# Scaled float16 halves for the second expert's input layer, with its x tiles loaded and scaled in groups of four

## The chip, the cores and the metric

The kernel runs on one core of one Trainium2 chip. The metric is the device time of one execution in microseconds (us). The engines are PE (TensorE: matmuls, with its weight loads shown apart as PEld), DVE (VectorE), ACT (ScalarE), POOL (GpSimd) and SP (SyncE, which issues the DMAs here).

## The reference

Three layers follow each other: block-causal attention (8 batches, 8 heads, 576 positions, head size 64), an expert with an ELU, and a second expert with a softmax-weighted unit and a layer norm. The diff touches the first product of the last one.

```python
x = attn_out.transpose(0, 2, 1, 3).reshape(4608, 512)
x = elu(x @ w_in) @ w_out                     # first expert, d_ff 2048
h = x @ w_in2                                 # second expert, d_ff 1024
e = exp(h - max(h)); sm = e / (sum(e) + 1e-9)
solu = h * sm
ln = (solu - mean(solu)) / sqrt(var(solu) + 1e-6) * g_ln
out = ln @ w_out2                             # [4608, 512], float32
```

The weights come in as 64-bit floats and are decoded to float32 on the chip.

## The kernel before

**Products in halves.** A float32 operand is split into a high and a low half, and a product of two operands is three matmuls: high by high, high by low and low by high. In attention, in the first expert and in the last product (`g4`, L1579) the halves are float16, scaled by a power of two or a bound on the values beforehand; in the second expert's input layer (`g3`, L1516) they are float32r, without a scale.

**The second expert.** It works on 36 tiles of 128 tokens. For a tile, SP loads x from the DRAM buffer `x2d` (`x_load`, L1499), ACT and DVE split it (`x_hi` L1504, `x_lo` L1508), and PE runs `g3`: 24 matmuls of 128x512. Then come `s_max` (L1523, DVE), `s_exp` (L1529, ACT), `s_solu` (L1534 to L1538, DVE), `s_var` (L1544, ACT), `s_rstd` (L1552, POOL), `s_ln` (L1556, DVE), `s_hi` and `s_lo` (L1561 on POOL, L1565 on DVE), and a transposing DMA (`s_tr`, L1571). Three tiles later `g4` (24 float16 matmuls of 128x512) multiplies the transposed halves with `w_out2`; ACT evicts (`o_ev`, L1587) and SP stores.

**Weights of the second expert.** While PE works on the last batches of the first expert, eight blocks are decoded: four of `w_in2` (`w3_*`) and four of `w_out2` (`w4_*`). A block is loaded into one of two buffers `r`, and goes through `dec_abs` (L773, ACT), `dec_sign` (L777, POOL), `dec_clamp` (L780, DVE) and `dec_bits` (L784 and L785, DVE) into a float32 block in one of two buffers `t3`. Of `w_in2`, each block is then split at once (`w3_hi` L1446 on ACT, `w3_lo` L1449 on DVE). Of `w_out2`, each block is multiplied by `g_ln` (L1468), reduced (`w4_amax`, L1472), the reductions are summed over the partitions by a small float32 matmul with ones (`over_partitions`, L285, a pair of PE instructions), DVE makes the scale (`w4_scale`), and the block is split (L1486, L1490).

**First expert.** `g1` (L683) makes eight pieces of a half batch, 24 matmuls each; ACT, DVE and POOL turn a piece into the float16 halves of G (L693, L695, L738, L742, L747), and `g2` (L757) needs pieces 0 to 3 for its first and 4 to 7 for its second half of the contraction.

**Order.** All instructions are issued in an order that a planner in the kernel works out when the kernel is built. Each operation has a cost, a due time (`nom`) and what it depends on; the planner keeps a clock for each engine and gives an engine that comes free, of the operations that could start first, the one with the lowest due time. Buffers and PSUM slots are rings (`Ring`); `rM` holds the four PSUM slots that all matmul groups share. The order is fixed: on the chip an engine waits where its next operation is not ready. The operations of the second expert have later due times than all of the first one's.

```python
rX, rXH, rXL, rE2, rSQ, rHL, rLT, rOS = Ring(2), Ring(2), Ring(2), Ring(3), Ring(2), Ring(2), Ring(LAG + 1), Ring(3)
```

Of the kernel before, what the change touches and what calls it, by code (L numbers as in the profile page):

```python
# [8 lines left out]
F32 = mybir.dt.float32  # L9
F32R = mybir.dt.float32r  # L10
# [22 lines left out]
LAG = 3  # L33
# [70 lines left out]
class Plan:  # L104
# [5 lines left out]
    def op(self, eng, cost, fn, nom, *deps, lat=0.12, dma=0.0):  # L110
        o = Op(eng, cost, fn, nom, deps, lat, dma, len(self.ops))
        self.ops.append(o)
        return o
# [87 lines left out]
def kernel(  # L201
# [732 lines left out]
    def cA(n, ap=1, acc=0, psum=False):  # L934
        return (0.834 * n + (52 if psum else 93) + 93 * ap + 93 * acc) / 1e3
# [475 lines left out]
    def open_p2():  # L1411
        es_att.close()
        w = ctx.enter_context(tc.tile_pool(name="p2w", bufs=1))
        p2["w3h"] = w.tile([128, 4, 1024], F32R, name="w3h")
        p2["w3l"] = w.tile([128, 4, 1024], F32R, name="w3l")
        p2["w4"] = w.tile([128, 8, 2, 512], F16, name="w4")
        p2["gl"] = w.tile([128, 8], F32, name="gl")
        p2["c4"] = w.tile([128, 3, 4], F32, name="c4")
        p2["mh"] = w.tile([128, 1], F32, name="mh")
        p2["px"] = w  # L1420
        p2["es_st"] = ExitStack()
        p2["st"] = p2["es_st"].enter_context(tc.tile_pool(name="p2st", bufs=1))
        SP.dma_start(out=p2["gl"], in_=g_ln.rearrange("(k p) -> p k", p=128))
# [9 lines left out]
        SP.dma_start(out=r, in_=w_in2.bitcast(I32)[128 * i:128 * i + 128].rearrange("p (f w) -> p f w", w=2))  # L1433

    def w3_abs(i):
        p2["t3", i] = p2["st"].tile([128, 1024], F32, name="t3", tag="t3", bufs=2)
        dec_abs(p2["t3", i], p2["r3", i])

    def w3_clamp(i):
# [2 lines left out]
    def w3_dec(i):  # L1442
        dec_bits(p2["t3", i], p2["r3", i])

    def w3_hi(i):
        A.activation(out=p2["w3h"][:, i], in_=p2["t3", i], func=AF.Copy, scale=1.0)  # L1446

    def w3_lo(i):
        V.tensor_tensor(out=p2["w3l"][:, i], in0=p2["t3", i], in1=p2["w3h"][:, i].bitcast(F32), op=ALU.subtract)  # L1449

    def w4_load(i):
        r = p2["st"].tile([128, 8, 128, 2], I32, name="r", tag="r", bufs=2)
# [1 line left out]
        SP.dma_start(out=r, in_=w_out2.bitcast(I32)[:, 256 * i:256 * i + 256].rearrange("(k p) (f w) -> p k f w", p=128, w=2))  # L1454

    def w4_abs(i):
        p2["t4", i] = p2["st"].tile([128, 8, 128], F32, name="t3", tag="t3", bufs=2)
        dec_abs(p2["t4", i], p2["r4", i])

    def w4_clamp(i):  # L1460
# [29 lines left out]
        V.scalar_tensor_tensor(out=p2["w4"][:, :, 1, 128 * i:128 * i + 128], in0=p2["t4", i], scalar=p2["c4"][:, 1, i:i + 1],  # L1490
                               in1=p2["w4"][:, :, 0, 128 * i:128 * i + 128], op0=ALU.mult, op1=ALU.subtract)

    x_t, h_t = {}, {}
    XB = 128

    def x_load(j):
        px = p2["px"]
        x = px.tile([128, 4, XB], F32, name="x", tag="x", bufs=2)
        SP.dma_start(out=x, in_=x2d[:, XB * j:XB * j + XB].rearrange("(k p) n -> p k n", p=128))  # L1499
        x_t[j] = [x, None, None]  # L1500

    def x_hi(j):
        x_t[j][1] = p2["px"].tile([128, 4, XB], F32R, name="xh", tag="xh", bufs=2)
        A.activation(out=x_t[j][1], in_=x_t[j][0], func=AF.Copy, scale=1.0)  # L1504

    def x_lo(j):
        x_t[j][2] = p2["px"].tile([128, 4, XB], F32R, name="xl", tag="xl", bufs=2)
        V.tensor_tensor(out=x_t[j][2], in0=x_t[j][0], in1=x_t[j][1].bitcast(F32), op=ALU.subtract)  # L1508

    def g3(i, slot):  # L1510
        _, xh, xl = x_t[i]
# [8 lines left out]
    def s_max(i):  # L1520
        d = h_t[i]
        d["mx"] = sm(1, "mx2")
        V.tensor_reduce(out=d["mx"], in_=d["h"], axis=AX.X, op=ALU.max, negate=True)  # L1523

    def s_exp(i):
        d = h_t[i]
        d["e"] = p2["wk"].tile([128, 1024], F32, name="e2", tag="e2", bufs=3)
        d["su"] = sm(1, "su2")
        A.activation(out=d["e"], in_=d["h"], func=AF.Exp, bias=d["mx"], scale=1.0, accum_out=d["su"])  # L1529

    def s_solu(i):
        d = h_t[i]
        r = sm(1, "r2")
        V.tensor_scalar(out=r, in0=d["su"], scalar1=1e-9, scalar2=None, op0=ALU.add)  # L1534
        V.reciprocal(out=r, in_=r)
        d["mu"] = sm(1, "mu")
        V.scalar_tensor_tensor(out=d["e"], in0=d["e"], scalar=r, in1=d["h"], op0=ALU.mult, op1=ALU.mult, accum_out=d["mu"])
        V.tensor_scalar(out=d["mu"], in0=d["mu"], scalar1=-1.0 / 1024.0, scalar2=None, op0=ALU.mult)  # L1538
# [60 lines left out]
        o = op("SP", DMA_IN, lambda: fn(i), nom, o_open, d, dma=dL(1048576))  # L1599
        return o, rR.users[-1]  # L1600

    w3_end, w4_end, prev = [], [], {}
    for i in range(8):
        z = i % 4
        t_ = t + 6 * i
        l, users = plan_load(w3_load if i < 4 else w4_load, z, t_ - 7)
        fa, fc, fd = (w3_abs, w3_clamp, w3_dec) if i < 4 else (w4_abs, w4_clamp, w4_dec)
        a_ = op("ACT", cA(1024, 0), lambda z=z, fa=fa: fa(z), t_, l, prev.get(i - 2))
        sg = op("Pool", 1.55, lambda z=z, i=i: dec_sign(p2["r3" if i < 4 else "r4", z]), t_ + 0.4, a_)
        x = op("DVE", 0.7, lambda z=z, fc=fc: fc(z), t_ + 0.5, a_)  # L1610
        x = op("DVE", 3.0, lambda z=z, fd=fd: fd(z), t_ + 1, x, sg)
        users += [a_, x]
        if i < 4:
            h = op("ACT", cA(1024, 0), lambda z=z: w3_hi(z), t_ + 4, x)
            lo = op("DVE", cV(1024, 0), lambda z=z: w3_lo(z), t_ + 5, h)
            w3_end += [h, lo]
        else:
            x = op("DVE", cV(1024, 0), lambda z=z: w4_g(z), t_ + 3, x, o_open)
            x = op("DVE", cV(1024, 0), lambda z=z: w4_amax(z), t_ + 4, x)
            x, users2 = plan_all(lambda y, z=z: w4_all(z, y), t_ + 5, x)  # L1620
            x = op("DVE", 0.7, lambda z=z: w4_scale(z), t_ + 5.5, x)
            users2.append(x)
            h = op("ACT", cA(1024, 1), lambda z=z: w4_hi(z), t_ + 6, x)
            lo = op("DVE", cV(1024, 1), lambda z=z: w4_lo(z), t_ + 7, h)
            w4_end += [h, lo]
        prev[i] = [h, lo]
    all_g2 = [x2_ops[b] for b in range(B)]
    t = tick(28 + 16 * 7) + 16 * TICK1
    o_openw = op("Pool", 0.01, open_wk, t, all_g2)
    rX, rXH, rXL, rE2, rSQ, rHL, rLT, rOS = Ring(2), Ring(2), Ring(2), Ring(3), Ring(2), Ring(2), Ring(LAG + 1), Ring(3)  # L1630
    xs_op = {}

    def plan_x(j, nom):
        lo_b, hi_b = (XB * j) // S, (XB * j + XB - 1) // S
        d = rX.take()
        l = op("SP", DMA_IN, lambda: x_load(j), nom - 10, o_open, d, [x2_ops[b] for b in range(lo_b, hi_b + 1)], dma=dL(512 * XB))
        d = rXH.take()
        h = op("ACT", cA(4 * XB, 0), lambda: x_hi(j), nom - 5, l, d)
        d = rXL.take()
        lo = op("DVE", cV(4 * XB, 0), lambda: x_lo(j), nom - 4, h, d)  # L1640
        rX.use(h, lo)
        xs_op[j] = lo

    T2 = 10.8
    g4s = []

    def plan_g4(i, nom):
# [6 lines left out]
        dz.users.append(ev)  # L1654
        rOS.use(op("SP", DMA_IN, lambda: o_st(i), nom + 6, ev, dma=dL(262144)))

    plan_x(0, t)
    for i in range(NTILE):
        nom = t + T2 * i
        if i + 1 < NTILE:  # L1660
            plan_x(i + 1, nom + T2)
        d = rM.take()
        mm = op("PE", 5.57, lambda i=i, d=d: g3(i, d), nom, xs_op[i], w3_end, d, chain[-1:])
        rXH.users[i].append(mm)
        rXL.users[i].append(mm)
        hu = d.users
# [62 lines left out]
```

## Time and profile before

| what | value |
|---|---|
| median of 3 runs | 1514.84 us (1513.22 to 1521.68) |
| profiled execution | 1522.49 us, of which the span from first to last instruction is 1520.7 us |
| mean granted clock of TensorE | 0.972 of full speed |
| busy: PE, DVE, ACT, POOL | 1444.7, 1052.5, 812.6, 536.3 us |
| busy of PE's weight loads (PEld) | 1022.1 us |

The busy share is a mean over stages with different limits. Matmuls are pipelined: one that is shown as busy for 379 ns can start its successor long before it ends, so a step is read from start to start or from the chain that ended last. Idle time counts only on the engine that sets the end.

### The profile page before, as it was taken

What the parts mean: (1) busy time and instruction counts of PE and PEld (TensorE: products, weight loads), DVE (VectorE), ACT (ScalarE), POOL (GpSimd) and SP (SyncE); (2) the same over time, 40 slices, a digit from 0 to 9 for tenths busy, and PEclk for the clock granted to TensorE, in tenths of its full rate; (3) what the DMA queues carried; (4) which work ended last, traced back from release to release, by engine and by line L of the source; (5) the groups of instructions that cost most, each with busy time, mean ns of one, the idle gap of its engine ahead of it and who ended that gap; (6) DMA issues with size and microseconds to landing.
All of it is one profiled execution on the core that took longest, in us unless ns stands there. A gap on an engine that the chain in (4) does not pass through costs nothing. (4 is left out here: it accounts for less than half of the span.)

```text
span 1520.7 us, 31276 instructions
## 1 busy us (share of the span) xinstructions
PE 1444.7 (95%) x12266; PEld 1022.1 (67%) x12268; DVE 1052.5 (69%) x1946; ACT 812.6 (53%) x1712; POOL 536.3 (35%) x631
## 2 busy tenths in 40 slices
PE   6888898999999999999999999989999999999998
PEld 3455565686777677678668667858776666666664
DVE  5879899878697787868868677597217555555552
ACT  4678666657475575565746656444414343333332
POOL 5677567444243343434424334242102111111110
PEclk9888799999999999999999999989999999999999
DMA  9235566856656576577565645530005444444433
GB/s 273 55 98 124 124 133 125 156 110 130 131 104 118 110 128 129 96 138 142 95 140 92 116 87 90 169 126 10 15 25 118 96 98 100 95 102 98 99 83 76
DMA packets 500130, 165.62 MB, mean 109 GB/s; under 512 B 445712, under 2 KB 492816, under 8 KB 499472
## 3 DMA queue, kind: packets, MB, share of 16 engines
q1 hardware_dynamic: 499984, 163.64, 50.7%
q8 instruction: 96, 1.57, 0.4%
q14 instruction: 50, 0.41, 0.1%
HBM read 63.44 MB, written 18.87 MB: 54 GB/s over the span
## 5 line engine op out<-in xcount | busy, mean ns | idle before, releaser
L683 PE MATMUL m<-XT,WIN 128*128 128x320 f16 (+1 forms) x3072 | 402.0, 289 | 10.5 <-DVE pwi L848 5.4
L757 PE MATMUL m<-G,WOUT 128*128 128x320 f16 (+1 forms) x3072 | 404.9, 291 | 5.2 <-POOL G L742 2.2
L683 PEld LDWEIGHTS <-WIN 128*128 128x128 f16 x3072 | 298.1, 99 | 96.1 <-issue 16.7
L757 PEld LDWEIGHTS <-WOUT 128*128 128x128 f16 x3072 | 298.8, 100 | 92.8 <-issue 8.7
L521 POOL TENSOR_SCALAR PN<-e,r 128x384 f16<-128x384 f32 (+2 forms) x280 | 184.7, 673 | 263.0 <-DVE r L503 120.3
L497 ACT ACTIVATE e<-m,nb,cqk 128x256 f32<-128x256 f32 (+4 forms) x252 | 159.7, 640 | 134.4 <-DVE nb L480 116.2
L742 POOL TENSOR_SCALAR G<-rp,sg 128x640 f16<-128x640 f32 (+1 forms) x128 | 126.6, 990 | 248.4 <-DVE rp L738 135.5
L693 ACT ACTIVATE rp<-m,ch 128x512 f32<-128x512 f32 (+1 forms) x256 | 176.4, 738 | 67.1 <-PE m L683 52.3
L1579 PE MATMUL m<-w,lt 128*128 128x512 f16 x864 | 192.2, 379 | 0.0
L526 DVE SCALAR_TENSOR_TENSOR PN<-e,r,PN 128x384 f16<-128x384 f32 (+2 forms) x280 | 172.3, 653 | 17.7 <-POOL PN L521 17.6
L1579 PEld LDWEIGHTS <-lt 128*128 128x128 f16 x864 | 81.9, 98 | 103.3 <-issue 8.9
L747 DVE SCALAR_TENSOR_TENSOR G<-rp,sg,G 128x640 f16<-128x640 f32 (+1 forms) x128 | 119.7, 938 | 26.2 <-POOL G L742 25.9
L476 DVE TENSOR_REDUCE mx<-m 128x2 f32<-128x768 f32 (+3 forms) x128 | 101.6, 814 | 44.5 <-PE m L452 37.8
L1552 POOL TENSOR_TENSOR rs<-vs,mh 128x1 f32<-128x1 f32 x36 | 20.9, 579 | 305.5 <-DVE vs L1547 305.5
L1516 PE MATMUL m<-w3h,xh 128*128 128x512 f32 x288 | 119.6, 415 | 0.0
L1516 PE MATMUL m<-w3h,xl 128*128 128x512 f32 x288 | 113.8, 395 | 0.0
L1516 PE MATMUL m<-w3l,xh 128*128 128x512 f32 x288 | 113.6, 394 | 0.0
L738 DVE SCALAR_TENSOR_TENSOR rp<-rp 128x512 f32<-128x512 f32 (+1 forms) x112 | 86.1, 769 | 33.3 <-ACT rp L695 32.7
L695 ACT ACTIVATE rp<-rp 128x640 f32<-128x640 f32 (+1 forms) x128 | 87.7, 685 | 2.0
L1523 DVE TENSOR_REDUCE mx<-m 128x1 f32<-128x1024 f32 x36 | 44.1, 1224 | 61.1 <-PE m L1516 61.1
L1504 ACT ACTIVATE xh<-x 128x512 fp32r<-128x512 f32 x36 | 22.5, 629 | 117.1 <-issue 112.8
L764 ACT ACTIVATE y<-m,ge 128x256 f32<-128x256 f32 (+1 forms) x64 | 28.4, 495 | 102.1 <-PE m L757 98.4
(169 smaller groups left out, 1901.1 us busy)
## 6 DMA issues: line engine op xcount, KB each, us to landing
x<-x2d SPq DMA_DIRECT2D x36, 256.0 KB, 3.0
out_dram<-o SPq DMA_DIRECT2D x36, 256.0 KB, 2.0
L<-in_k_dram SPq DMA_DIRECT2D x68, 128.0 KB, 2.6
WOUT<-in_moe_w_in_dram SPq DMA_DIRECT2D x8, 1024.0 KB, 6.4
LV<-in_v_dram SPq DMA_DIRECT2D x64, 128.0 KB, 2.8
XT<-in_moe_w_out_dram SPq DMA_DIRECT2D x16, 512.0 KB, 4.4
L<-in_q_dram SPq DMA_DIRECT2D x60, 128.0 KB, 2.6
x2d<-y SPq DMA_DIRECT2D x32, 160.0 KB, 2.0
```

The costliest lines, as they stand in the source:

```text
L476: V.tensor_reduce(out=mx[:, 2 * j:2 * j + 2], in_=s.S[:, :, s.off[i]:s.off[i] + 128 * (i + 1)], axis=AX.X, op=ALU.max)
L497: A.activation(out=dst, in_=src, func=AF.Exp, scale=s.sc()[1], bias=s.nb[:, x:x + 1], accum_out=s.su[:, x:x + 1])
L521: P.tensor_scalar(out=h, in0=e, scalar1=s.r[:, x:x + 1], scalar2=1.0, op0=ALU.mult, op1=ALU.mult)
L526: V.scalar_tensor_tensor(out=l, in0=e, scalar=s.r[:, x:x + 1], in1=h, op0=ALU.mult, op1=ALU.subtract)
L683: E.matmul(out=t[:, m, 0:n], lhsT=WIN[:, kk, wl, f:f + 128], rhs=x[:, kk, xl, o:o + n], start=kk == 0 and wl + xl == 0, stop=kk == 3 and w ...
L693: A.activation(out=d[1 + w][:, :, 0:n], in_=d[0][:, :, 0:n], func=AF.Relu, scale=ch[:, 4 * w + g:4 * w + g + 1])
L695: A.activation(out=d[2][:, :, 0:n], in_=d[2][:, :, 0:n], func=AF.Exp, scale=-1.0)
L742: P.tensor_scalar(out=GV[:, 2 * c:2 * c + 2, 0, 0:n], in0=mo_t[b, h, c][1][:, :, 0:n], scalar1=bs_t[b]["sg"], scalar2=1.0, op0=ALU.mult, o ...
L747: V.scalar_tensor_tensor(out=GV[:, 2 * c:2 * c + 2, 1, 0:n], in0=mo_t.pop((b, h, c))[1][:, :, 0:n], scalar=bs_t[b]["sg"], in1=GV[:, 2 * c: ...
L757: E.matmul(out=t[:, d % 2, 0:n], lhsT=WOUT[:, kk, wl, 128 * d:128 * d + 128], rhs=GV[:, kk, xl, 0:n], start=kk == 0 and wl + xl == 0, stop ...
L1516: E.matmul(out=t[:, nn], lhsT=a[:, kk], rhs=w[:, kk, 512 * nn:512 * nn + 512], start=kk == 0 and a is xh and w is p2["w3h"], stop=kk == 3 ...
L1579: E.matmul(out=t, lhsT=d["lt"][:, 8 * xl + kk, :], rhs=p2["w4"][:, kk, wl, :], start=kk == 0 and xl + wl == 0, stop=kk == 7 and xl == 1)
```

## The change

The halves of `w_in2` and x become float16. `w_in2` gets one scale for all of it: each decoded block is reduced (`w3_amax`), and when all four are there, one `over_partitions` (`w3_all`) and `w3_scale` make the scale, and only then are the four blocks split; the ring of `t3` has four buffers. x tiles are loaded four at a time into a ring of eight buffers; each tile is reduced (`x_amax`, DVE), the four reductions are summed over partitions by one `over_partitions` (`x_all`, PE), and `x_scale` makes for each tile the scale, its inverse together with the one of the weights (`c`) and `ci` for the softmax sum. `s_max`, `s_exp` and `s_solu` take these factors as operands: one more small DVE instruction in `s_max`. The planner's costs and the due times' spacing (`T2`) follow.

```diff
...
         w = ctx.enter_context(tc.tile_pool(name="p2w", bufs=1))
-        p2["w3h"] = w.tile([128, 4, 1024], F32R, name="w3h")
-        p2["w3l"] = w.tile([128, 4, 1024], F32R, name="w3l")
+        p2["w3h"] = w.tile([128, 4, 1024], F16, name="w3h")
+        p2["w3l"] = w.tile([128, 4, 1024], F16, name="w3l")
+        p2["am3"] = w.tile([128, 4], F32, name="am3")
+        p2["c3"] = w.tile([128, 3], F32, name="c3")
         p2["w4"] = w.tile([128, 8, 2, 512], F16, name="w4")
...
     def w3_abs(i):
-        p2["t3", i] = p2["st"].tile([128, 1024], F32, name="t3", tag="t3", bufs=2)
+        p2["t3", i] = p2["st"].tile([128, 1024], F32, name="t3", tag="t3", bufs=4)
         dec_abs(p2["t3", i], p2["r3", i])
...
+    def w3_amax(i):
+        V.tensor_reduce(out=p2["am3"][:, i:i + 1], in_=p2["t3", i], axis=AX.X, op=ALU.max, apply_absolute_value=True)
+    def w3_all(slot):
+        p2["ar3"] = over_partitions(p2["am3"], 4, slot)
+    def w3_scale():
+        c = p2["c3"]
+        V.tensor_reduce(out=c[:, 0:1], in_=p2["ar3"], axis=AX.X, op=ALU.max)
+        pow2(c[:, 0:1], c[:, 0:1], 2.0 ** -100)
+        scale_of(c[:, 1:2], c[:, 0:1], 2.0 ** 14)
+        V.tensor_scalar(out=c[:, 2:3], in0=c[:, 0:1], scalar1=2.0 ** -14, scalar2=None, op0=ALU.mult)
     def w3_hi(i):
-        A.activation(out=p2["w3h"][:, i], in_=p2["t3", i], func=AF.Copy, scale=1.0)
+        A.activation(out=p2["w3h"][:, i], in_=p2["t3", i], func=AF.Copy, scale=p2["c3"][:, 1:2])
     def w3_lo(i):
-        V.tensor_tensor(out=p2["w3l"][:, i], in0=p2["t3", i], in1=p2["w3h"][:, i].bitcast(F32), op=ALU.subtract)
+        V.scalar_tensor_tensor(out=p2["w3l"][:, i], in0=p2["t3", i], scalar=p2["c3"][:, 1:2], in1=p2["w3h"][:, i],
+                               op0=ALU.mult, op1=ALU.subtract)
...
     def w4_abs(i):
-        p2["t4", i] = p2["st"].tile([128, 8, 128], F32, name="t3", tag="t3", bufs=2)
+        p2["t4", i] = p2["st"].tile([128, 8, 128], F32, name="t3", tag="t3", bufs=4)
         dec_abs(p2["t4", i], p2["r4", i])
...
-    x_t, h_t = {}, {}
+    x_t, h_t, xs_t = {}, {}, {}
     XB = 128
+    XG = 4
     def x_load(j):
-        px = p2["px"]
-        x = px.tile([128, 4, XB], F32, name="x", tag="x", bufs=2)
+        x = p2["px"].tile([128, 4, XB], F32, name="x", tag="x", bufs=2 * XG)
         SP.dma_start(out=x, in_=x2d[:, XB * j:XB * j + XB].rearrange("(k p) n -> p k n", p=128))
...
+    def x_amax(j):
+        if j % XG == 0:
+            xs_t[j // XG] = [sm(XG, "xa")]
+        V.tensor_reduce(out=xs_t[j // XG][0][:, j % XG:j % XG + 1], in_=x_t[j][0].rearrange("p k n -> p (k n)"), axis=AX.X,
+                        op=ALU.max, apply_absolute_value=True)
+    def x_all(y, slot):
+        xs_t[y].append(over_partitions(xs_t[y][0], XG, slot))
+    def x_scale(y):
+        p = xs_t[y][1]
+        t, s, c, ci = (sm(XG, tag) for tag in ("xt", "xs", "xc", "xi"))
+        V.tensor_scalar(out=t, in0=p, scalar1=2.0 ** -60, scalar2=2.0 ** -14, op0=ALU.max, op1=ALU.mult)
+        V.reciprocal(out=s, in_=t)
+        V.tensor_scalar(out=c, in0=t, scalar1=p2["c3"][:, 2:3], scalar2=None, op0=ALU.mult)
+        V.tensor_scalar(out=ci, in0=s, scalar1=p2["c3"][:, 1:2], scalar2=None, op0=ALU.mult)
+        xs_t[y] = (s, c, ci)
+    def x_sc(j, n):
+        return xs_t[j // XG][n][:, j % XG:j % XG + 1]
     def x_hi(j):
-        x_t[j][1] = p2["px"].tile([128, 4, XB], F32R, name="xh", tag="xh", bufs=2)
-        A.activation(out=x_t[j][1], in_=x_t[j][0], func=AF.Copy, scale=1.0)
+        x_t[j][1] = p2["px"].tile([128, 4, XB], F16, name="xh", tag="xh", bufs=2)
+        A.activation(out=x_t[j][1], in_=x_t[j][0], func=AF.Copy, scale=x_sc(j, 0))
     def x_lo(j):
-        x_t[j][2] = p2["px"].tile([128, 4, XB], F32R, name="xl", tag="xl", bufs=2)
-        V.tensor_tensor(out=x_t[j][2], in0=x_t[j][0], in1=x_t[j][1].bitcast(F32), op=ALU.subtract)
+        x_t[j][2] = p2["px"].tile([128, 4, XB], F16, name="xl", tag="xl", bufs=2)
+        V.scalar_tensor_tensor(out=x_t[j][2], in0=x_t[j][0], scalar=x_sc(j, 0), in1=x_t[j][1], op0=ALU.mult, op1=ALU.subtract)
...
         V.tensor_reduce(out=d["mx"], in_=d["h"], axis=AX.X, op=ALU.max, negate=True)
+        V.tensor_scalar(out=d["mx"], in0=d["mx"], scalar1=x_sc(i, 1), scalar2=None, op0=ALU.mult)
...
         d["su"] = sm(1, "su2")
-        A.activation(out=d["e"], in_=d["h"], func=AF.Exp, bias=d["mx"], scale=1.0, accum_out=d["su"])
+        A.activation(out=d["e"], in_=d["h"], func=AF.Exp, bias=d["mx"], scale=x_sc(i, 1), accum_out=d["su"])
...
         r = sm(1, "r2")
-        V.tensor_scalar(out=r, in0=d["su"], scalar1=1e-9, scalar2=None, op0=ALU.add)
+        V.tensor_scalar(out=r, in0=d["su"], scalar1=1e-9, scalar2=x_sc(i, 2), op0=ALU.add, op1=ALU.mult)
         V.reciprocal(out=r, in_=r)
...
-    w3_end, w4_end, prev = [], [], {}
+    w3_end, w4_end, w3_am, t3_free = [], [], [], []
     for i in range(8):
...
         fa, fc, fd = (w3_abs, w3_clamp, w3_dec) if i < 4 else (w4_abs, w4_clamp, w4_dec)
-        a_ = op("ACT", cA(1024, 0), lambda z=z, fa=fa: fa(z), t_, l, prev.get(i - 2))
+        a_ = op("ACT", cA(1024, 0), lambda z=z, fa=fa: fa(z), t_, l, t3_free[i - 4] if i >= 4 else None)
         sg = op("Pool", 1.55, lambda z=z, i=i: dec_sign(p2["r3" if i < 4 else "r4", z]), t_ + 0.4, a_)
...
         if i < 4:
-            h = op("ACT", cA(1024, 0), lambda z=z: w3_hi(z), t_ + 4, x)
-            lo = op("DVE", cV(1024, 0), lambda z=z: w3_lo(z), t_ + 5, h)
-            w3_end += [h, lo]
+            w3_am.append(op("DVE", cV(1024, 0), lambda z=z: w3_amax(z), t_ + 3, x))
+            h = lo = None
+            if i == 3:
+                x, users2 = plan_all(w3_all, t_ + 3.5, w3_am)
+                o_w3s = op("DVE", 0.7, w3_scale, t_ + 4, x)
+                users2.append(o_w3s)
+                for y in range(4):
+                    h = op("ACT", cA(1024, 1), lambda y=y: w3_hi(y), t_ + 4.1, o_w3s)
+                    lo = op("DVE", cV(1024, 1), lambda y=y: w3_lo(y), t_ + 5, h)
+                    w3_end += [h, lo]
+                    t3_free.append([h, lo])
         else:
...
             w4_end += [h, lo]
-        prev[i] = [h, lo]
     all_g2 = [x2_ops[b] for b in range(B)]
...
     o_openw = op("Pool", 0.01, open_wk, t, all_g2)
-    rX, rXH, rXL, rE2, rSQ, rHL, rLT, rOS = Ring(2), Ring(2), Ring(2), Ring(3), Ring(2), Ring(2), Ring(LAG + 1), Ring(3)
+    rX, rXH, rXL, rE2, rSQ, rHL, rLT, rOS = Ring(2 * XG), Ring(2), Ring(2), Ring(3), Ring(2), Ring(2), Ring(LAG + 1), Ring(3)
     xs_op = {}
+    def plan_xs(y, nom):
+        ld, am, users = [], [], []
+        for j in range(XG * y, XG * y + XG):
+            lo_b, hi_b = (XB * j) // S, (XB * j + XB - 1) // S
+            d = rX.take()
+            ld.append(op("SP", DMA_IN, lambda j=j: x_load(j), nom - 12, o_open, d, [x2_ops[b] for b in range(lo_b, hi_b + 1)],
+                         dma=dL(512 * XB)))
+            users.append(rX.users[-1])
+            am.append(op("DVE", cV(4 * XB, 0), lambda j=j: x_amax(j), nom - 9, ld[-1]))
+        o, mu = plan_all(lambda z: x_all(y, z), nom - 7, am)
+        o = op("DVE", 0.3, lambda: x_scale(y), nom - 6.5, o, o_w3s)
+        mu.append(o)
+        for j in range(XG * y, XG * y + XG):
+            xg_op[j] = (o, users[j - XG * y])
+    xg_op = {}
     def plan_x(j, nom):
-        lo_b, hi_b = (XB * j) // S, (XB * j + XB - 1) // S
-        d = rX.take()
-        l = op("SP", DMA_IN, lambda: x_load(j), nom - 10, o_open, d, [x2_ops[b] for b in range(lo_b, hi_b + 1)], dma=dL(512 * XB))
+        o, users = xg_op[j]
         d = rXH.take()
-        h = op("ACT", cA(4 * XB, 0), lambda: x_hi(j), nom - 5, l, d)
+        h = op("ACT", cA(4 * XB, 1), lambda: x_hi(j), nom - 5, o, d)
         d = rXL.take()
-        lo = op("DVE", cV(4 * XB, 0), lambda: x_lo(j), nom - 4, h, d)
-        rX.use(h, lo)
+        lo = op("DVE", cV(4 * XB, 1), lambda: x_lo(j), nom - 4, h, d)
+        users += [h, lo]
         xs_op[j] = lo
-    T2 = 10.8
+    T2 = 10.4
     g4s = []
...
+    plan_xs(0, t)
     plan_x(0, t)
...
         nom = t + T2 * i
+        if i % XG == 0 and i + XG < NTILE:
+            plan_xs(i // XG + 1, nom + 2.5 * T2)
         if i + 1 < NTILE:
...
         d = rM.take()
-        mm = op("PE", 5.57, lambda i=i, d=d: g3(i, d), nom, xs_op[i], w3_end, d, chain[-1:])
+        mm = op("PE", 24 * cE(512), lambda i=i, d=d: g3(i, d), nom, xs_op[i], w3_end, d, chain[-1:])
         rXH.users[i].append(mm)
...
         hu = d.users
```

## Rows read from the trace of the kernel before

**Rows 1.** The page: busy time by engine, and DVE's slices of the span.

```profile
PE 1444.7 (95%) x12266; PEld 1022.1 (67%) x12268; DVE 1052.5 (69%) x1946; ACT 812.6 (53%) x1712; POOL 536.3 (35%) x631
...
DVE  5879899878697787868868677597217555555552
```

**Rows 2.** The chain that ended last, from 1055 us: start, us, what, how many.

```profile
1055.04 20.96 PE m L757 x192
...
1102.08 26.08 PE m L757 x192
1128.15 22.29 PE m L1516 x96
1150.45 5.20 PE m L1579 x24
1155.64 5.59 PE m L1516 x24
...
1495.41 16.27 PE m L1579 x76
```

**Rows 3.** Windows: PE, PEld, DVE, ACT, POOL busy us, granted clock, DMA share, GB/s.

```profile
955.00:978.00 23.00, 23.00 (x242) 19.37 (x241) 7.83 (x8) 8.27 (x13) 3.25 (x2) 1.00 0.68 213
...
998.00:1010.00 12.00, 9.28 (x65) 6.24 (x64) 11.35 (x12) 5.42 (x7) 6.51 (x4) 0.95 0.28 98
1010.00:1019.00 9.00, 7.20 (x33) 4.15 (x33) 8.93 (x8) 1.58 (x3) 1.37 (x1) 0.69 0.40 125
...
1161.00:1494.00 333.00, 333.00 (x1485) 209.55 (x1484) 178.55 (x310) 126.61 (x278) 49.34 (x62) 1.00 0.43 96
```

**Rows 4.** Timeline of PE: start, us, instruction, how many, idle before and releaser.

```profile
997.57 9.34 PE L757 MATMUL m<-G,WOUT 128*128 128x320 f16 x66
1009.13 0.42 PE L757 MATMUL m<-G,WOUT 128*128 128x320 f16 x1 [2.22 <-POOL G L742]
1010.04 6.77 PE L757 MATMUL m<-G,WOUT 128*128 128x320 f16 x29 [0.50 <-DVE G L747]
1018.57 0.35 PE L285 MATMUL m<-amo,ones 128*128 128x1 f32 x2 [1.76 <-DVE amo L1472]
1018.79 5.09 PE L757 MATMUL m<-G,WOUT 128*128 128x320 f16 x24
...
1033.63 5.40 PE L683 MATMUL m<-XT,WIN 128*128 128x256 f16 x48
```

**Rows 5.** Timeline of all engines at the end of the span.

```profile
1495.25 20.89 PE L1579 MATMUL m<-w,lt 128*128 128x512 f16 x96
...
1505.33 1.93 SPq L1571 DMA_TRANSPOSE lt<-hl  x1
```

**Rows 6.** Groups by line, 1161.24 to 1473.85: busy us, mean ns, idle before.

```profile
L1579 PE MATMUL m<-w,lt 128*128 128x512 f16 x697 | 155.7, 379 | 0.0
...
L1579 PEld LDWEIGHTS <-lt 128*128 128x128 f16 x696 | 65.8, 98 | 83.3 <-issue 8.1
L1516 PEld LDWEIGHTS m<-w3l,xh 128*128 128x128 f32 x232 | 43.7, 188 | 9.9
...
L1523 DVE TENSOR_REDUCE mx<-m 128x1 f32<-128x1024 f32 x29 | 35.5, 1224 | 30.9 <-PE m L1516 30.9
...
L1508 DVE TENSOR_TENSOR xl<-x,xh 128x512 fp32r<-128x512 f32 x29 | 19.7, 681 | 0.0
...
L1538 DVE TENSOR_SCALAR mu<-mu 128x1 f32<-128x1 f32 x29 | 4.5, 153 | 1.0
```

**Rows 7.** Timeline of PE around a reduction over partitions.

```profile
1040.76 1.04 PE L683 MATMUL m<-XT,WIN 128*128 128x256 f16 x8
...
1041.78 0.81 PE L683 MATMUL m<-XT,WIN 128*128 128x256 f16 x6
```

**Rows 8.** Timeline of SP: the first transpose of the last stage.

```profile
1145.43 1.73 SPq L1571 DMA_TRANSPOSE lt<-hl  x1
```

**Rows 9.** The line of the transposes, all 36: issue to landing.

```profile
DMA to landing us min/median/max: 4.2/4.3/5.6
```

## The prediction

> **What bounds the kernel now.** I read the page first, then the chain that ended last, then windows and timelines of the two stretches that the diff touches. On the page TensorE (PE) is busy 95% of the span, VectorE (DVE) 69%, and DVE's slices thin out to 5 in the last quarter [rows 1]. That average hides two regimes, so the chain comes next.
>
> From 1128.15 us to the end the chain is PE and nothing else: 96 matmuls of the second expert's input layer (L1516, four tiles at once) in 22.29 us, then 32 pairs of one output layer (L1579, 24 matmuls) and one input layer (24 matmuls), then the last output layers [rows 2]. From 1150.45 to 1495.41 that is 344.96 us for 32 pairs, 10.780 us each. In the same stretch DVE is busy 178.55 of 333 us, ACT 126.61, POOL 49.34, at a granted clock of 1.00 [rows 3]: nothing but PE limits this stage, and a matmul that gets shorter shows up in the end at full size.
>
> The other stretch is the end of the first expert layer, where the second layer's weights are decoded. In 192 matmuls of 128x320, batch 6's second half takes 997.57 to 1033.63 [rows 4]; the same work for batch 7 takes 26.08 us [rows 2]. So about 10 us are lost there. [...] The slow clock is nearly half of the loss: 29 matmuls in 6.77 us and 24 in 5.09 [rows 4], where 26.08/192 = 0.136 is the full pace [rows 2], is 2.8 + 1.8 = 4.6 us. DVE is the engine that is late there.
>
> **The change part by part.** *Halves in float16 (g3).* A float32r matmul of 512 columns steps at 22.29/96 = 0.2322 us. A float16 one of the same shape is already in the trace: the last 96 output matmuls are busy 20.89 us [rows 5], less the 0.38 us that the last one is busy by itself [rows 6], over 95 steps: 0.2159 us. A pair of all float16 is 48 x 0.2159 = 10.363 us. That saves 10.780 - 10.363 = 0.417 us in 32 pairs (13.3 us) and 22.29 - 96 x 0.2159 = 1.6 us in the first four tiles: 14.9 us. Lower bound: the chain's own shares, 5.585 and 5.195 us, give 0.39 x 36 = 14.0.
>
> The weight load of a float32r matmul takes 188 ns, that of a float16 one 98 [rows 6]. [...]
>
> *Reductions over partitions (x_all, w3_all).* Nine plus one pairs of small float32 matmuls enter PE's stream. The rows of L285 show one between float16 matmuls: eight of 128x256 from 1040.76 (step 20.96/192 = 0.109 [rows 2]) put the last start at 1041.52, and the pair is followed by a next one 0.26 us later [rows 7] instead of 0.11, so 0.15 us for a pair, 1.5 us for ten. Bounds: nothing (hidden under a 512-column matmul, 0.216) and the 0.35 us of a pair that came after a wait [rows 4]: 0 to 3.5 us. They have 4 columns where the rows have 1, which I take as free. In the last stage each x_all stands behind its four x_amax by more than three tiles, because the loads of a group start when the group before last gives its buffers back, so I expect no wait of PE there.
>
> *DVE's new work in the last stage.* Per tile x_amax (128x512): between half of a 128x1024 reduction, 1.22/2, and the 0.68 us of today's x_lo (L1508), taken as 0.65; the product on mx 0.15 [rows 6], and four such small operations per group, 0.15 a tile. DVE goes from 178.55 x 10.78/333 = 5.8 to 6.7 us of a 10.4 us tile, so PE's stream covers it; without the cover it would be 0.95 us a tile. x_lo and x_hi keep their shapes; ACT at 38% [rows 3] takes a scale operand without being felt. Eight x buffers in place of two only move loads earlier on SP's queue, behind which stand the transposes that feed L1579. These have three tiles of slack. If a load lands late, DVE waits in x_amax with s_max and s_solu behind it, and these hold a PSUM slot; g3 and g4 each need about one slot of the four at a time, so it costs nothing up to several us.
>
> *Start of the last stage.* Here the cover is thin. Four g3 in a row take 96 x 0.2159, so PE is ready for the first g4 at 1148.9 instead of 1150.4. Its transpose was issued at 1145.43 and lands 4.2 to 5.6 us later [rows 8, 9], that is just before g4 began. DVE gets 0.15 to 1.5 us more before that transpose, while g3(0) ends 0.4 us earlier. The wait is 0 (if the planner puts a fifth g3 first) to 2.5 us; I take 1.0. At the end the last transpose, issued 10.1 us after the last g3 [rows 5], still lands about a microsecond before its g4.
>
> *Weights of w_in2.* Before, each of four blocks was split by ACT and DVE as soon as decoded; now four reductions, one matmul pair, six small operations, and only then hi and lo. On DVE, amax (1.22 us, by the reduction of that size [rows 6]) takes lo's place, lo comes later, and w4_abs of the first block now waits for the first lo. Up to 1055 us DVE gets 4 x 1.22 (w3_amax) + 8 x 0.65 (x_amax of two groups, whose loads fit the eight buffers) + 6 x 0.15 + 2 x 4 x 0.15 + 0.3 = 12.4 us more. What covers it: DVE is busy 7.83 of 23 us before 978 [rows 3], and from 1055 on the chain is PE alone [rows 2]. What does not: 978 to 1024. Behind the waiting DVE operations on its queue stand the G halves (L747), for which PE waits, and w3_all and x_all now stand in PE's stream as w4_all did when PE waited 1.76 us. Bounds: -10.1 (the moved splits free DVE, the whole loss goes) and +12.4 (all of it passes to PE). The planner lets G's work go first and fills gaps with the rest, and amax replaces lo one for one in the critical stretch, so I take 0, with 4 us either way as my estimate.
>
> *Sum:* -14.9 + 1.5 + 1.0 + 0 = -12.4 us. The profiled execution took 1522.49 us (span 1520.7 plus 1.8), so it would be 1510.1. The median of the three runs is 1514.84, 7.65 below the profiled one; I take the same difference from it: 1502.4 us.
>
> **The rivals.**
> - *The weights' end pays part of it.* One more wait of PE in 1000 to 1030 for w3_all or a late G, with a slow clock behind it as there is now [rows 3, 4]: 1.8 + 4.6 = 6.4 us, with 5 to 10 as my estimate of its scatter. For it: DVE is at 99% there. Against it: 15 us of idle DVE before 978 can take the x_amax. Time: 1507 to 1512.
> - *DVE's backlog passes on to PE whole (slower).* All 12.4 us, and two more stretches of slow clock at 4.6 each, 21.6 us, at the G halves of batch 6 and again of batch 7 at 1055: 1502.4 + 21.6 = 1524.0. It is slower by over 0.5% once more than 20 us pass on. Against it: G has priority in the order, and DVE has little to do after 1055.
> - *The new order removes the old wait.* Without ACT's four splits between g1's evictions, G comes in time: -5 to -10, 1492 to 1497.
> - *The change doesn't do what it says.* Float16 input matmuls step like float32r ones: only the costs remain, 1514.84 + 2.5 = 1517.3. Against it: 697 float16 matmuls of this very shape in the steady stretch alone [rows 6].
>
> **How the numbers follow.** Chances: forecast 0.62 (own range 1498 to 1507), weights' end pays 0.20, old wait removed 0.10, backlog passes on 0.05, no effect 0.03. The range 1495 to 1512 holds all of the first, nearly all of the second and about half of the third, some 0.85. A measurement here tells about 0.5%, 7.6 us, from no change (the three runs spread over 8.5 us). Faster than 1507.3: 0.59 of the first, a fifth of the second, all of the third, 0.73. Same: 0.03 + 0.16 + 0.03 = 0.22. Slower: 0.05.
>
> **What would show it.** Right: on the chain of waits, L1516 x24 at 5.18 us instead of 5.585 and pairs of about 10.37; PEld for L1516 at 98 ns; L285 seven to nine times after 1060 with no wait before it; PE's granted clock 1.00 to the end; the first g4 within 2.5 us of the fourth g3. For the weights' end: the first L1516 starts within 4 us of 1128.15 in a run whose earlier part takes the same time. Wrong: PE idle on L285 or on L757 between 990 and 1060, a granted clock below 0.9 for longer than it is now, or float16 input matmuls stepping above 0.225 us.

## The result, and the profile after

The changed kernel takes 1497.51 us (median of 4 runs, 1490.88 to 1502.03) beside 1518.26 us for the kernel before (median of 4, 1513.22 to 1521.82): a ratio of 0.9849 with a 95% interval of 0.9816 to 0.9882. The forecast was a gain of 12.4 us, to 1502.4; the medians are 20.8 us apart, and by the ratio the gain is 17.9 to 27.9 us. The time lies in the range of 1495 to 1512, but the gain is clear of the forecast's, so something is missing from the sum. The forecast's 1502.4 started from a median of 1514.84, and the median before is now 1518.26; so the time came out 4.9 us from the forecast and the gain 8.4. One run of the experiments, 1820.26 us of the kernel with PN moved, was slow, and is in that kernel's median but not in its ratio. The profiled execution takes 1495.12 us (span 1493.3), 27.4 us less than the one of before.

The page of the kernel after: busy time by engine, and DVE's slices, as in [rows 1].

```profile
PE 1420.7 (95%) x12288; PEld 943.9 (63%) x12288; DVE 1090.9 (73%) x2064; ACT 820.8 (55%) x1712; POOL 536.3 (36%) x631
...
DVE  5889899888687777878868677498318566666553
```

DVE has 38 us more, most of it in the last quarter, where its slices went from 5 to 6. Shares don't tell where the time went; marks on the chain do. The chain that ended last of the kernel after, as in [rows 2]: start, us, what, how many.

```profile
946.47 10.59 PE m L757 x96
...
1113.65 25.90 PE m L1553 x120
1139.55 10.36 PE m L1617 x48
1149.91 5.18 PE m L1553 x24
1155.09 5.18 PE m L1617 x24
1160.27 0.12 PE m L285 x2
1160.39 5.20 PE m L1553 x24
...
1466.85 11.07 PE m L1617 x52
...
1478.89 4.20 DMA lt<-hl
```

The same view of the kernel before has this line for the first mark:

```profile
961.06 10.59 PE m L757 x96
```

These 96 matmuls are the first half of batch 6's `g2`, ahead of all work on the second expert's weights: SP issues the first load of it at 946.78 us in the kernel after. Three stretches follow:

| stretch | before | after | difference | forecast |
|---|---|---|---|---|
| start to the first mark | 961.06 | 946.47 | -14.6 | 0 |
| mark to the first `g3` (1128.15 and 1113.65) | 167.1 | 167.2 | +0.1 | 0, 4 either way |
| first `g3` to the end of the span | 392.55 | 379.65 | -12.9 | -14.9 + 1.0 + some 1.0 for seven `x_all` |

The last stage did what the sum said, within 0.1 us. The end of the first expert cost what it cost before. Over half of the gain of this execution was made ahead of everything that the diff adds, where PE runs the same instructions in the same order.

The last stage in detail. Groups by line of the kernel after, 1149.91 to 1456.49, to be read against [rows 6]:

```profile
L1553 PE MATMUL m<-w3l,xh 128*128 128x512 f16 x240 | 90.9, 379 | 0.0
...
L1553 PEld LDWEIGHTS <-xh 128*128 128x128 f16 x478 | 46.8, 99 | 54.8
...
L1545 DVE SCALAR_TENSOR_TENSOR xl<-x,xs,xh 128x512 f16<-128x512 f32 x29 | 21.6, 744 | 0.0
...
L1521 DVE TENSOR_REDUCE xa<-x 128x1 f32<-128x512 f32 x22 | 15.1, 685 | 25.6 <-DMA x<-x2d 25.4
L1561 DVE TENSOR_SCALAR mx<-mx,xc 128x1 f32<-128x1 f32 x29 | 6.2, 214 | 1.0
```

The weight load of a `g3` matmul fell from 188 to 99 ns and its step from 0.2322 to 25.90/120 = 0.2158 us. The operations that take an operand per partition cost a little more: the product on mx takes 0.21 us where 0.15 was taken, and `x_lo`, now with a product in it, 0.74 where it took 0.68 (with float16 halves alone the mean of all 36 is 0.71, the same as in the kernel before, so it isn't the type).

Windows of the kernel after (PE, PEld, DVE, ACT, POOL busy us, granted clock, DMA share, GB/s), as in [rows 3]: the wait in the weights' end, what follows it, and the steady stage.

```profile
1004.00:1009.00 5.00, 0.00 (x0) 0.00 (x0) 4.97 (x5) 0.00 (x0) 0.00 (x0) 0.89 0.87 275
1009.00:1019.00 10.00, 9.68 (x54) 6.43 (x55) 9.76 (x19) 3.44 (x3) 2.96 (x2) 0.71 0.32 108
1146.00:1466.00 320.00, 320.00 (x1494) 146.18 (x1492) 201.19 (x390) 132.71 (x281) 50.65 (x64) 1.00 0.43 97
```

DVE is busy 201.19 x 10.37/320 = 6.5 us of a tile and PE all of it, at full clock. The last `x_amax` is at 1370 us; in the 16 tiles from 1160.30 to 1326.50, each with an `x_amax`, DVE is busy 106.09/16 = 6.6 us a tile (6.7 forecast). Timeline of PE in the weights' end, as in [rows 4]:

```profile
990.15 0.36 PE L285 MATMUL m<-am,ones 128*128 128x4 f32 x2 [0.49 <-DVE am L1448]
990.37 13.32 PE L757 MATMUL m<-G,WOUT 128*128 128x320 f16 x96
1009.32 0.56 PE L285 MATMUL m<-amo,ones 128*128 128x1 f32 x2 [5.63 <-DVE amo L1488]
1009.74 5.88 PE L757 MATMUL m<-G,WOUT 128*128 128x320 f16 x24
```

The waits for G [rows 4] are gone. In their place PE stands 5.63 us before the `over_partitions` of the first `w_out2` block, while DVE is busy 4.97 of the 5 us from 1004 on, and the next ten microseconds run at a granted clock of 0.71: it reads 0.50 in each us from 1009 to 1014, 0.61 in the next and 1.00 from 1015 on. In the kernel before it reads 0.50 in each us from 1010 to 1015, 0.74 in the next and 1.00 from 1016 to 1018, which is the slow clock that the prediction counts [rows 3]. The half batch takes 982.98 to 1018.85, 35.9 us, where it took 36.1. All waits of PE from 920 us to the end, in us, times and longest:

```profile
PE m L285 <- DVE amo L1488: 5.6, 1, 5.6
PE m L1617 <- DMA lt<-hl: 1.0, 1, 1.0
PE m L563 <- DMA PT<-PN: 0.7, 1, 0.7
PE m L285 <- DVE am L1448: 0.5, 1, 0.5
```

The 1.0 us that the sum put at the first `g4` stands before the last one: the planner put a fifth `g3` first (x120 on the chain), and the last transpose was issued at 1478.89, 12.2 us after the last `g3` gave way at 1466.68, where it was 10.1.

### The profile page after: what moved, and what is told of

Same layout as the page of the kernel before. It is cut to its first block, busy times and chain, and to the rows that moved or that the text cites. A ratio compares the mean times of both kernels' runs of the same rounds, so it can differ in the third digit from the quotient of the medians.

```text
span 1493.3 us, 31436 instructions
## 1 busy us (share of the span) xinstructions
PE 1420.7 (95%) x12288; PEld 943.9 (63%) x12288; DVE 1090.9 (73%) x2064; ACT 820.8 (55%) x1712; POOL 536.3 (36%) x631
## 3 DMA queue, kind: packets, MB, share of 16 engines
q8 instruction: 97, 1.59, 0.5%
## 5 line engine op out<-in xcount | busy, mean ns | idle before, releaser
L1553 PE MATMUL m<-w3h,xl 128*128 128x512 f16 x288 | 109.1, 379 | 0.0
L1553 PE MATMUL m<-w3l,xh 128*128 128x512 f16 x288 | 109.1, 379 | 0.0
L1553 PE MATMUL m<-w3h,xh 128*128 128x512 f16 x288 | 109.1, 379 | 0.0
L1553 PEld LDWEIGHTS <-xh 128*128 128x128 f16 x576 | 56.4, 99 | 66.1
L1567 ACT ACTIVATE e<-m,mx,xc 128x1024 f32<-128x1024 f32 x36 | 43.3, 1204 | 62.2 <-DVE mx L1561 58.1
```

The source lines that it names most:

```text
L1553: E.matmul(out=t[:, nn], lhsT=a[:, kk], rhs=w[:, kk, 512 * nn:512 * nn + 512], start=kk == 0 and a is xh and w is p2["w3h"], stop=kk == 3 ...
```

## The experiments

**What made the first 946 us shorter.** One of the DMAs that PE waits for in attention differs between the traces: the transpose of P (`tr`, L550: PT from PN). The line of these 56 transposes, before and then after: duration of the issue on SP's queue in ns (min, median, max), first and last start, and issue to landing.

```profile
L550 SPq DMA_TRANSPOSE PT<-PN x56: 3502/3905/4702, 196.6 to 952.0; - x56
...
DMA to landing us min/median/max: 5.4/5.9/7.5
```

```profile
L550 SPq DMA_TRANSPOSE PT<-PN x56: 2942/3270/4557, 192.3 to 938.3; - x56
...
DMA to landing us min/median/max: 4.5/5.2/7.0
```

The diff doesn't touch them, but it moves them. `sm` puts five new small tiles with four buffers each into the pool `small`; at 32 bytes per partition each, the pools that are opened behind it on the same side of SBUF start 640 bytes later. PN went from byte 41600 of its partition (128 past a multiple of 256) to 42240 (a multiple), PT from 82560 to 83200. Theory: the shift itself is worth the 12 us or so that the sum lacks. Rivals: scatter between executions, or something else in the changed program. Three kernels tell these apart: before with the shift alone, by 640 and by 128 bytes, and after without it.

```diff
+    pad = const.tile([128, 160], F32, name="pad"); es_moe = ExitStack()   # before; [128, 32] for 128 bytes
...
+    def xsm(tag):                                                          # after: out of the pool small
+        return p2["px"].tile([128, XG], F32, name=tag, tag=tag, bufs=4)
```

> The kernel before with an unused tile of 640 bytes per partition ahead of the attention pool; nothing else differs. Theory (address shift): the new small tiles of the change moved the attention tiles by 640 bytes, and the transposing DMA PT<-PN became cheaper by that alone (median issue 3.91 to 3.27 us, landing 5.9 to 5.2); then this kernel shows about 3.3 and 5.2 us, the start of the 96 matmuls of batch 6's first output half comes near 946 to 953 us instead of 961, and the time is 5 to 11 us below that of the kernel before. Rival (scatter): the upstream part differs from run to run and the rest of the result is chance; then the transposes stay at 3.9 and 5.9 us and the time is within 4 us of the kernel before.

> As the run with 640 bytes, with 128 bytes. If what counts is that PT begins at a multiple of 256 bytes (the size of a block's row of 128 float16), 128 bytes do the same as 640: transposes at 3.3 and 5.2 us, 5 to 11 us faster. If it is a property of the shift by 640 alone, or scatter, the transposes stay near 3.9 us and the time within 4 us of the kernel before.

> The changed kernel with the five scale tiles of x in the second expert's pool instead of the small one, so that the attention tiles lie where they lay before. Address shift: transposes back at 3.9 and 5.9 us, and the time is what the prediction's sum gives without that gift, 12 us below the kernel before (ratio 0.990 to 0.994). Scatter: no difference to the changed kernel, ratio about 0.985.

Before with 640 unused bytes takes 1507.39 us, ratio 0.9918 (0.9898 to 0.9939); with 128 bytes 1507.96, ratio 0.9929 (0.9906 to 0.9952). No instruction was changed. The changed kernel without the shift takes 1508.33, ratio 0.9919 (0.9899 to 0.9939): a gain of 12.3 us by that ratio, the forecast's 12.4. Its first mark is back at 960.30, its mark to first `g3` is 166.9 and its last stage 379.7. The two ratios multiplied, 0.9918 x 0.9919 = 0.984, give the whole change. The shift by 640 bytes is worth 12.5 us by its ratio, more than the 5 to 11 that were expected of it. The transposes follow the address; of the changed kernel without the shift:

```profile
L550 SPq DMA_TRANSPOSE PT<-PN x56: 3512/3902/4825, 195.6 to 951.1; - x56
...
DMA to landing us min/median/max: 5.5/5.9/7.6
```

How that reaches PE shows in part in its waits from 190 to 945 us for the two kinds of transposes that SP issues in attention, before and then before with 640 bytes:

```profile
PE m L449 <- DMA QKT<-N: 6.8, 8, 1.5
PE m L563 <- DMA PT<-PN: 6.4, 5, 2.1
```

```profile
PE m L449 <- DMA QKT<-N: 3.6, 4, 1.6
PE m L563 <- DMA PT<-PN: 2.6, 4, 1.0
```

They fall by 7.0 us, and the next wait for PT, at 950, from 1.59 to 0.72. That is 7.9 of the 14.3 us by which the first mark moves between these two traces (961.06 to 946.72); through which waits the rest comes is not shown.

**Which tile it is.** Before, with 128 bytes ahead of PT only, which moves PT and N behind it; ahead of PN and again ahead of PT (which moves PN and its neighbours by 128 and PT by 256); and ahead of PN and right behind it, so that PN alone changes its place within 256 bytes.

```diff
+    pad0 = att.tile([128, 32], F32, name="pad0")                           # second and third kernel
     PN = [att.tile([128, 26, 128], F16, name=f"PN{i}") for i in range(2)]
+    pad1 = att.tile([128, 32], F32, name="pad1")                           # third kernel
...
+            pads.append(att.tile([128, 32], F32, name="pad"))              # once, ahead of PT: first and second
```

> The kernel before with 128 unused bytes directly ahead of PT in the attention pool: PT (the transposes' destination) now begins at a multiple of 256 bytes, PN (their source) stays 128 bytes off one. If the destination's address makes the difference: median issue about 3.3 us, landing 5.2, and the whole 12 us of the two earlier shifts. If the source's does: 3.9 and 5.9 us, and no gain beyond 3 us.

> The counterpart: 128 unused bytes ahead of PN and 128 more ahead of PT, so that the source begins at a multiple of 256 bytes and the destination stays 128 off. Destination theory: 3.9 and 5.9 us, time within 3 us of the kernel before. Source theory: 3.3 and 5.2 us and some 12 us faster.

> The kernel before with 128 unused bytes ahead of PN and 128 behind it: only PN, the source of the transposes, changes its place within 256 bytes; VS, QKT, e, PT and N move by 256 and keep theirs. If PN's place alone makes the difference: median issue near 3.27 us, landing near 5.0, and the same 10 to 13 us as the shifts of all tiles. If VS, QKT or e had a part in it, the transposes or the time stay between, less than 8 us faster.

PT alone: 1520.5 us, ratio 1.0001 (0.9983 to 1.0019), so the destination's place, 0 or 128 past a multiple, made no difference. With PN moved: 1506.38 us, ratio 0.9898 (0.9876 to 0.9921). PN only: 1507.87 us, ratio 0.9919 (0.9897 to 0.9942). The line of the transposes, with PT moved and then with PN only:

```profile
L550 SPq DMA_TRANSPOSE PT<-PN x56: 3508/3890/5161, 193.5 to 952.2; - x56
...
DMA to landing us min/median/max: 5.4/5.9/7.6
```

```profile
L552 SPq DMA_TRANSPOSE PT<-PN x56: 2962/3286/5654, 192.4 to 934.2; - x56
...
DMA to landing us min/median/max: 4.6/5.1/7.6
```

For these transposes the place of the source decided: 3.9 us of SP's queue against 3.3 for each, and 0.8 us sooner landing. For short transposes it was worth little: the 140 of `QKT` from `N` (L353), 4 blocks of 128 columns each where those of PN have 24 or 26, have their source on a multiple of 256 with PT alone moved, and 128 past one with PN moved. Their issue takes 1264 ns (median) in both, and they land 0.1 us apart (as in the kernels before, 128 past, and after, on a multiple: 1264 ns in both, 2.5 and 2.4 us), with PT alone moved and then with PN moved:

```profile
DMA to landing us min/median/max: 2.3/2.4/5.8
```

```profile
DMA to landing us min/median/max: 2.3/2.5/5.1
```

A row of one 128x128 block of PN, 128 float16 values, is 256 bytes long. Here a source at 128 past a multiple of 256 bytes cost 0.6 us of issue and 0.8 of landing, and a destination there nothing (1.0001); how the transposes are read no run here shows.

**The halves by themselves.** The kernel before with float16 halves and nothing else of the change; it leaves out the scaling of both operands.

```diff
-        p2["w3h"] = w.tile([128, 4, 1024], F32R, name="w3h")
+        p2["w3h"] = w.tile([128, 4, 1024], F16, name="w3h")
...
-        x_t[j][1] = p2["px"].tile([128, 4, XB], F32R, name="xh", tag="xh", bufs=2)
+        x_t[j][1] = p2["px"].tile([128, 4, XB], F16, name="xh", tag="xh", bufs=2)
```

> The kernel before with float16 halves of w_in2 and x and nothing else: no scale, no groups, no reductions, attention tiles where they were. This leaves out the scaling, so the low halves are less exact. The prediction's term for the matmuls alone: 14.9 us faster (ratio 0.990), pairs of 10.363 us on the chain, and about 2.4 us below the changed kernel without the address shift (1508.3). Rival: the reductions and the later splits cost nothing or help, then it is no faster than that kernel.

1507.28 us, ratio 0.9902 (0.988 to 0.9925): 14.9 us of 1518.95 (11.4 to 18.2 by the interval). The last stage, 1126.95 to 1505.2, takes 378.25 us, 14.3 less than before; scale and groups cost 379.7 - 378.25 = 1.4 us there, the seven `x_all` of 0.13 and the wait at the end, less a wait of 0.6 at the first `g4` that this kernel has.

**The wait in the weights' end.** Theory: the matmul of the first `w_out2` block's reduction stands too early in PE's order, and due later it costs 7 to 9 us less. Rival: DVE's backlog is what counts, and the next reduction stands in its place.

```diff
-    def plan_all(fn, nom, o):
+    def plan_all(fn, nom, *o):
...
+            x, users2 = plan_all(lambda y, z=z: w4_all(z, y), t_ + 5, x, chain[32 * (B - 1) + 3 + 2 * z])
```

> The changed kernel with the four reductions of w_out2 over partitions (w4_all) ordered behind later matmul groups of batch 7. Theory: PE's 5.63 us wait for amo at 1003.7 and the slow clock behind it (24 matmuls in 5.74 instead of 3.28 us) are one loss of about 8 us, and it goes: 7 to 9 us faster than the changed kernel, ratio to the kernel before about 0.980. Rival: DVE is late anyway and PE meets the next wait for it (G of batch 7, or a later reduction): under 3 us.

1495.83 us, ratio 0.9839 (0.9818 to 0.9859), which can't be told from the changed kernel's 0.9849. The timeline of PE shows the wait for amo gone and this one in its place; mark to first `g3` is 1112.19 - 944.80 = 167.4 us. The theory fell.

```profile
1022.63 0.56 PE L285 MATMUL m<-xa,ones 128*128 128x4 f32 x2 [6.28 <-DVE xa L1521]
```

So DVE's work itself was moved: decoding of the `w_out2` blocks starts only after given pieces of the last batch, and the first `x_all` later too. A third kernel also adds 224 unused bytes to the last stage's pool, by which all of the pool starts 224 bytes lower: hl, the source of that stage's transposes, goes from byte 198624 to 198400, a multiple of 256, and lt, their destination, from 206816 to 206592, a multiple too.

```diff
+        late = chain[32 * (B - 1) + (8, 11, 24, 27)[z]] if i >= 4 else None
+        a_ = op("ACT", cA(1024, 0), lambda z=z, fa=fa: fa(z), t_, l, t3_free[i - 4] if i >= 4 else None, late)
...
+        o, mu = plan_all(lambda z: x_all(y, z), nom - 7, am, chain[32 * (B - 1) + 12])
...
+            p2["padw"] = p2["wk"].tile([128, 56], F32, name="padw")        # the third kernel only
```

> The changed kernel with the decoding of the four w_out2 blocks started only at batch 7's second product and the x_all of the first two groups behind it, so that nothing of PE's stream in front of batch 7 waits for DVE's backlog. If the some 9 us that batch 6's second half loses are all due to that backlog, PE runs from batch 6's g1 to the last stage in about 158 instead of 167 us and the time is 8 to 9 us below the changed kernel (near 1488). If one more wait takes their place (G of batch 7, or a reduction further on), it is under 4 us.

> The version with w_out2 and x reductions late, with 224 unused bytes behind the last stage's tiles, so that hl, the source of that stage's transposes, begins at a multiple of 256 bytes instead of 32 below one. If a source's place within 256 bytes is what a transposing DMA's time hangs on, lt<-hl lands in 3.6 to 3.9 us instead of 4.3, as PT<-PN did from 5.9 to 5.1; PE's wait of 0.9 us for the last of them goes, and the time is 0.5 to 1.5 us below that version's 1486.0, which five rounds can hardly tell. If it is a property of PN or of the attention stage alone, lt<-hl stays at 4.3 us.

With the work moved: 1486.04 us, ratio 0.977 (0.9749 to 0.9791), faster than both kernels, 11.5 us below the changed kernel's median where 8 to 9 were expected. Mark to first `g3` is 943.60 to 1102.17, 158.6 us instead of 167.2; the first mark itself, ahead of the edit, comes 2.9 us earlier in this execution. Windows of it, and all waits of PE from 920 us on:

```profile
995.00:1004.00 9.00, 9.00 (x68) 6.46 (x66) 3.44 (x6) 0.23 (x1) 0.00 (x0) 1.00 0.11 38
1004.00:1012.00 8.00, 8.00 (x70) 6.63 (x68) 0.03 (x1) 2.85 (x5) 0.00 (x0) 1.00 0.12 41
```

```profile
PE m L1617 <- DMA lt<-hl: 0.9, 1, 0.9
PE m L563 <- DMA PT<-PN: 0.9, 1, 0.9
PE m L285 <- DVE am L1448: 0.4, 1, 0.4
```

PE doesn't stop, and the granted clock stays at 1.00. With the last pool moved as well: 1485.68 us, ratio 0.9769 (0.9755 to 0.9783). Its transposes land in 3.7 us instead of 4.3 (medians; 16 blocks of 128 columns each) and the last wait falls from 0.9 to 0.3, but the 0.4 us between the two kernels is less than a comparison can tell. The effect of the address is there, though this kernel doesn't tell source from destination; with three tiles of slack in front of each `g4` it buys next to nothing. The landing of these transposes, where [rows 9] have 4.2/4.3/5.6 for the kernel before:

```profile
DMA to landing us min/median/max: 3.6/3.7/5.2
```

**How far DVE's cover goes.** The changed kernel with each `x_amax` done four and eight times, one run each; the planner is told the cost.

```diff
+        for _ in range(4):                                                 # 8
+            V.tensor_reduce(out=xs_t[j // XG][0][:, j % XG:j % XG + 1], in_=x_t[j][0].rearrange("p k n -> p (k n)"), axis=AX.X,
+                            op=ALU.max, apply_absolute_value=True)
```

> The changed kernel with each x_amax done four times: 3 x 0.685 us more of DVE per tile, 6.5 + 2.1 = 8.6 us of a 10.36 us tile. If the scaling is covered by PE's stream as the prediction says, pairs stay at 10.36 us and the last stage is within 2 us of the changed kernel's 379.7; if DVE's added time reaches the end, the last stage grows by 2 us a tile, some 70 us.

> As before, eight times: DVE would need 6.5 + 7 x 0.685 = 11.3 us a tile, more than PE's 10.36. The cover is then gone: the last stage should grow to about 36 x 11.3 = 407 us or more, some 25 to 35 us longer, with PE waiting for DVE in its idle time. If it stays at 380, DVE was not what the cover argument took it for.

Four times: 1497.86 us; pairs stay at 10.36 us and the last stage takes 381.5 us, 1.9 more than after. The window of the same 16 tiles:

```profile
1160.30:1326.50 166.20, 166.20 (x775) 75.81 (x774) 138.35 (x254) 67.79 (x144) 24.75 (x30) 1.00 0.45 101
```

That is 8.6 us of DVE a tile. Eight times: 1543.56 us, last stage 409.1, 29.5 more. Waits of PE in its last stage, and DVE's `s_max` of three tiles:

```profile
PE m L1618 <- DMA lt<-hl: 12.0, 12, 2.8
PE m L1554 <- DVE vs L1586: 7.3, 1, 7.3
PE m L1554 <- DVE e L1576: 2.0, 5, 0.9
```

```profile
1212.92 1.22 DVE L1561 TENSOR_REDUCE mx<-m 128x1 f32<-128x1024 f32 x1
...
1224.38 1.22 DVE L1561 TENSOR_REDUCE mx<-m 128x1 f32<-128x1024 f32 x1
...
1235.83 1.22 DVE L1561 TENSOR_REDUCE mx<-m 128x1 f32<-128x1024 f32 x1
```

A tile takes 11.46 us, and 6.6 + 7 x 0.685 = 11.4 is what DVE then has to do in it. The cover holds at 8.6 us of DVE a tile and is gone at 11.4; PE's 10.4 lies between, and where between them it ends was not tried. The whole times hold more than that stage: mark to first `g3` takes 162.4 us with four and 187.4 with eight, where it took 167.2. With eight, the added work also costs PE 20 us in the weights' end, where its longest waits are 6.6 us for ACT's rp and 5.2 for DVE's am; that is the way of the prediction's second rival, but with much more work than the change has, and it was not followed further.

## Why the prediction was right, and what it missed

- *Halves in float16:* right. Step 0.2158 (forecast 0.2159), pairs 10.36 us (10.363). The halves alone took 14.9 us from the time by ratio and 14.3 from the last stage; 14.9 was forecast. The rival that nothing would step faster is refuted by the step and by the weight load, 188 to 99 ns.
- *Reductions over partitions:* the price was right, 0.12 to 0.14 us a pair (0.15), and no `x_all` from 1060 us on was waited for.
- *DVE's new work:* covered, as forecast, and the cover was measured: at 8.6 us of DVE a tile it holds, at 11.4 it is gone. The product on mx was mis-sized (0.15 for 0.21) without effect.
- *Start of the last stage:* the 1.0 us was in the wrong place. The case that the working allowed, a fifth `g3` first, made it 0 there; the step "still lands about a microsecond before its `g4`" failed, and 0.98 us is lost at the end. The total came out right by that exchange, which is luck. The sign "the first g4 within 2.5 us of the fourth g3" did not appear either: the first `g4` starts at 1139.55, 5.2 us behind it, because of the fifth `g3`, and PE doesn't wait.
- *Weights of `w_in2`:* net nothing, as taken, but not for the reason given. The waits for G went, and a wait of 5.63 us with a slow clock behind it came: parts of two rivals, which cancel; that they do so to 0.2 us (35.9 for 36.1) is luck. The prediction's own sign of being wrong, PE idle on L285 between 990 and 1060, appeared, and the stretch cost nothing more all the same. That the loss could be had was right too: 158.6 instead of 167.2 us once the decoding of `w_out2` and the first `x_all` are moved, 8.6 of the 10.1 that was the bound; which of the two moves counts was not told apart.
- *What failed:* the accounting of what the change moves. It followed instructions, queues and buffers and left out addresses. The step "x_lo and x_hi keep their shapes" and what stands beside it go through the new operations one by one, but nowhere does it say where the new tiles lie. There is no term for the 640 bytes, which were worth 12.5 us by ratio, as much as the whole sum. Without them the changed kernel gives the sum (0.9919, -12.3 us, with an interval of 9.3 to 15.4). That the changed kernel's time still lies in the stated range is partly luck: the range was wide, and the median that it was counted from was 3.4 us below that of the result. The third rival's time, 1492 to 1497, came close to the result by another mechanism than its own.

Open: why the transposes' source costs what it does inside the DMA engines, why the issue of the short ones from N doesn't feel it, and whether other places than those tried (0 and 128 past a multiple of 256 for PN, 0 and 224 for hl) behave like them. Also open: whether a float32r matmul steps slower for its weight load or for its other operand.

## What to carry to other kernels

Before a stage's gain is credited to an edit, compare marks ahead of the edit: a time that changed where no instruction did points to placement (here 14.6 us ahead of the first mark). An edit that allocates even a few small tiles moves the pools behind them (here five tiles, 640 bytes), so list the addresses of the sources of transposing DMAs before and after, and try to align those of the long ones that something waits for (here to a multiple of 256 bytes, which took 12 us off). When PE waits in order for a reduction of an engine that is behind, moving the matmul may only pass the wait on (here 5.63 us for amo became 6.28 for xa); move the backlog (here 8.6 us less up to the first `g3`).

## What the runs showed of the hardware

A transposing DMA from SBUF of 24 or 26 blocks of 128 float16 columns took 3.9 us on its queue with its source at 128 past a multiple of 256 bytes and 3.3 on a multiple, and landed in 5.9 against 5.1 us; 56 of them were worth 12 us of 1520. One of 16 blocks landed in 4.3 us with source and destination at 224 past a multiple, and in 3.7 with both on a multiple. One of 4 blocks landed in 2.5 us with its source at 128 past a multiple and in 2.4 on one, and its 1.26 us on the queue stayed. Per block that is 0.03, 0.04 and 0.03 us of landing, an estimate from these medians. The destination's place, 0 or 128 past a multiple, made no difference to the first kind (1.0001).
